# Loading a weight matrix as column halves, a reordered VectorE and an fp32 warm-up in a linear-attention kernel

## The chip, the core and the metric

The kernel runs on one core of a Trainium2 chip. A core has five engines, each with its own in-order instruction stream: TensorE (PE in the profile; its weight loads are PEld), VectorE (DVE), ScalarE (ACT), GpSimd (POOL) and SyncE (SP, which here only issues DMAs). Sixteen DMA engines move data between HBM and the on-chip memories. The metric is the device time of one execution in microseconds (us); lower is better.

## The reference

Input x has 2048 rows of 640 numbers (bf16). Each row is first normalized to xn. The result is x plus two branches of xn:

```python
xn = _layernorm(x)                       # mean and variance over the 640 columns
# A: linear attention with 32 heads of 20
q, k, v = split(xn @ wqkv)
phi = lambda t: where(t > 0, t + 1, exp(t)) + 1e-6
kv  = sum over rows of phi(k)^T v        # one 20x20 matrix per head
z   = sum over rows of phi(k)
A   = ((phi(q) @ kv) / (phi(q) . z + 1e-6)) @ wo
# B: the 8 rows with the largest r = xn @ w_r go through a small MLP
B   = xn, with sigmoid(r) * ((silu(x_sel @ w_gate) * (x_sel @ w_up)) @ w_down) added to those 8 rows
out = x + A + B
```

## The kernel before, in words

The rows are cut into 16 tiles of 128 rows, tile t being rows 128t to 128t+127. The program has a fixed order, written out by hand: every engine runs its instructions in the order in which the Python code emits them, and waits on semaphores for data of the other engines. All loads go through one queue that SyncE issues in order.

**First stage (0 to about 52 us in the profile).** For each tile:

- x arrives by DMA in `XX[:, t, 1, :]`.
- The statistics of a row: `ln_a` and `ln_b` are one `bn_stats` each, over half the columns (L145, L148, VectorE); `ln_g` joins them (L151); `ln_s` (L170, L172) makes the standard deviation with a power on GpSimd. For tiles 1 and 5 ScalarE makes the sums instead (`ln_act`, L159 to L161) and VectorE the variance (`ln_var`, L164).
- `ln_c` (L177 on ScalarE, L179 on VectorE) subtracts the mean, `ln_xn` (L184 a reciprocal, L186 a product) scales and writes the normalized tile.
- The normalized tile is transposed into `xnT`: for tiles 0 to 3 by TensorE, with a copy out of PSUM by ScalarE (`tr_pe`, L193 and L197), from tile 4 on by a DMA (`tr_dma`, L202) that SyncE issues.
- `K(t)` (L224) multiplies by the k weights `wk`: two halves h of 320 columns, 5 products each. The second half has a 321st column that holds w_r, so that r comes out beside k.
- `PHa(t)` (L240, L243, ScalarE) makes exp and relu of both halves, `PHb(t)` (L259, VectorE) joins them into phi(k), `pk`.
- `G(t)` (L264, L269) adds xn^T phi(k) up over the tiles in PSUM.

Tiles 0 to 3 are emitted one by one (L344 to L418); from tile 4 a loop (L419 to L445) emits `K(t)`, `PHb(t-1)`, the normalization of tile t+2, `PHa(t)`, the statistics of tile t+3, and `G(t-1)`. A transposed tile t+2 has thus to be there two rounds of the loop after its normalization was emitted. In the loop the first half statistic stands behind `PHb(t-1)` and ahead of `ln_xn(t+2)` for t = 4 to 8 (tile t+3), and at the round's end for t of 8 and more (tile t+4).

Before the first tile arrives TensorE runs products of zeros (`warm`, L116), and one small transposition of w_r (L127) whose result ScalarE later copies into the 321st column of `wk` (L362, L364). A few lines of the start, with their order:

```python
    ld(sp, XX[:, 2, 1, :], x_v[:, 2, :])
    ld(sp, wk[:, 0:3, 0:D], wqkv_v[:, 0:3, D : 2 * D])
    ld(sp, wk[:, 3:KC, 0:D], wqkv_v[:, 3:KC, D : 2 * D])
    warm(4)
    pe.transpose(PS[:, 5, :].bitcast(BF16)[:, 0:KC], wr[:], ident[0:KC, 0:KC])
    warm(5)
    ld(sp, XX[:, 3, 1, :], x_v[:, 3, :])
```

**Second stage (about 52 us to the end).** The q products (L455) with their exp and relu (L461, L462, L510), the matrices of the heads, the routing of 8 rows through the MLP, and last the output products (L686) tile by tile with the sum and the store (L700, L702). None of this is changed.

Of the kernel before, what the change touches and what calls it, by code (L numbers as in the profile page):

```python
# [7 lines left out]
P = 128  # L8
S = 2048
D = 640  # L10
# [3 lines left out]
T = S // P  # L14
KC = D // P
# [7 lines left out]
FQ = F // 4  # L23
EPS_BF16 = 1.0013580322265625e-05
LOW = S - 1
TF = 11

BF16 = mybir.dt.bfloat16
F32 = mybir.dt.float32
# [7 lines left out]
def kernel(  # L37
# [13 lines left out]
    pe, dve, act, pool, sp = nc.tensor, nc.vector, nc.scalar, nc.gpsimd, nc.sync  # L51

    x_v = A_x[0].rearrange("(t p) d -> p t d", p=P)
    out_v = out[0].rearrange("(t p) d -> p t d", p=P)
    wqkv_v = A_wqkv.rearrange("(kc p) n -> p kc n", p=P)
# [7 lines left out]
    PS = psp.tile([P, 8, 512], F32, name="PS")  # L63

    def st(shape, dt, name, tag=None):
        return sb.tile(shape, dt, name=name, tag=tag or name)

    XX = st([P, T, 2, D], BF16, "XX")
    xnT = st([P, KC, S], BF16, "xnT")
    pk = st([P, T, D], BF16, "pk", "pkwd")  # L70
    pqT = st([P, KC, S], BF16, "pqT")
    wk = st([P, KC, D + 1], BF16, "wk", "wkM")
    wq = st([P, KC, D], BF16, "wq")
    wo1 = st([P, NG, D], BF16, "wo1")
    wo2 = st([P, D], BF16, "wo2")
# [4 lines left out]
    zero = st([P, 512], BF16, "zero")  # L80
    ident = st([P, P], BF16, "ident")
# [12 lines left out]
    MR = st([P, T], F32, "MR")  # L94

    HW = 320


    def ld(eng, dst, src):
        eng.dma_start(dst, src)  # L100
# [5 lines left out]
    wr = st([KC, P], BF16, "wr")  # L106
    ld(act, wr[:], B_w_r.rearrange("(kc p) -> kc p", p=P))
    ld(sp, XX[:, 1, 1, :], x_v[:, 1, :])
    ld(sp, XX[:, 2, 1, :], x_v[:, 2, :])
    ld(sp, wk[:, 0:3, 0:D], wqkv_v[:, 0:3, D : 2 * D])  # L110
    ld(sp, wk[:, 3:KC, 0:D], wqkv_v[:, 3:KC, D : 2 * D])


    def warm(n, w=512):
        for _ in range(n):
            pe.matmul(PS[:, 7, 0:w], lhsT=zero[:, 0:P], rhs=zero[:, 0:w], start=True, stop=True)  # L116
# [6 lines left out]
    )  # L123
    dve.memset(ones32[:], 1.0)
    dve.memset(eps6[:], 1e-6)
    warm(4)
    pe.transpose(PS[:, 5, :].bitcast(BF16)[:, 0:KC], wr[:], ident[0:KC, 0:KC])  # L127
    warm(5)
    ld(sp, XX[:, 3, 1, :], x_v[:, 3, :])
    kv1 = st([P, NG, GC], BF16, "kv1")  # L130
    kv2 = st([P, NG, GC], BF16, "kv2")
    xsT = st([P, KC, 32], BF16, "xsT")
# [10 lines left out]
    def ln_a(t):  # L143
        sts[t] = tmp.tile([P, 2, nc.vector.BN_STATS_DIM], F32, tag="stats", name="stats", bufs=3)
        dve.bn_stats(out=sts[t][:, 0, :], in_=XX[:, t, 1, 0:320])  # L145

    def ln_b(t):
        dve.bn_stats(out=sts[t][:, 1, :], in_=XX[:, t, 1, 320:D])  # L148

    def ln_g(t):  # L150
        dve.bn_aggr(out=MV[:, t, :], in_=sts[t][:])  # L151
# [3 lines left out]
    sm = st([P, T, 2], F32, "sm")  # L155
    junk = st([P, D], BF16, "junk")

    def ln_act(t):
        act.activation(junk[:], XX[:, t, 1, :], AF.Identity, scale=1.0 / D, accum_out=sm[:, t, 0:1])  # L159
        act.copy(MV[:, t, 0:1], sm[:, t, 0:1])  # L160
        act.activation(junk[:], XX[:, t, 1, :], AF.Square, scale=float(D) ** -0.5, accum_out=sm[:, t, 1:2])  # L161

    def ln_var(t):
        dve.scalar_tensor_tensor(out=MV[:, t, 1:2], in0=sm[:, t, 0:1], scalar=sm[:, t, 0:1], in1=sm[:, t, 1:2],  # L164
                                 op0=ALU.mult, op1=ALU.subtract)

    def ln_s(t, sg=1.0):
        t2 = tmp.tile([P, 1], BF16, tag="t2", name="t2", bufs=4)
        ss[t] = tmp.tile([P, 1], BF16, tag="s", name="s", bufs=4)
        dve.tensor_scalar(out=t2[:], in0=MV[:, t, 1:2], scalar1=sg, scalar2=EPS_BF16,  # L170
                          op0=ALU.mult, op1=ALU.add)
        pool.tensor_tensor(out=ss[t][:], in0=t2[:], in1=halfc[:], op=ALU.pow)  # L172

    def ln_c(t, eng):
        cs[t] = tmp.tile([P, D], BF16, tag="c", name="c", bufs=3)
        if eng is act:
            act.activation(cs[t][:], XX[:, t, 1, :], AF.Identity, bias=MVf[:, t, 0:1], scale=-1.0)  # L177
        else:
            dve.tensor_scalar(out=cs[t][:], in0=XX[:, t, 1, :], scalar1=MVf[:, t, 0:1], scalar2=-1.0,  # L179
                              op0=ALU.subtract, op1=ALU.mult)  # L180
# [8 lines left out]
    def tr_pe(t, b0, e0, e1, hs=(0, 1)):  # L189
        for b, k0, k1, eng in [((b0, 0, 3, e0), (b0 + 1, 3, KC, e1))[h] for h in hs]:  # L190
            pt = PS[:, b, :].bitcast(BF16)[:, 0 : (k1 - k0) * P]
            for kc in range(k0, k1):
                pe.transpose(pt[:, (kc - k0) * P : (kc - k0 + 1) * P], XX[:, t, 0, kc * P : (kc + 1) * P], ident[:])  # L193
            dst = xnT[:, k0:k1, t * P : (t + 1) * P]
            src = pt.rearrange("p (k c) -> p k c", c=P)
            if eng is act:
                act.copy(dst, src)  # L197
            else:
                dve.tensor_copy(dst, src)
# [9 lines left out]
    def xpx(t):  # L209
        if t >= TF:  # L210
            dve.tensor_scalar(out=XX[:, t, 1, :], in0=XX[:, t, 1, :], scalar1=SR1[:, t : t + 1],
                              scalar2=MR[:, t : t + 1], op0=ALU.mult, op1=ALU.add)
            return
        act.activation(XX[:, t, 1, :], XX[:, t, 1, :], AF.Identity, bias=MR[:, t : t + 1], scale=SR1[:, t : t + 1])  # L214


    def off(t, h):
        return T - 1 - t if t != 1 and h else 0

    def K(t, hs=(0, 1), b=6, kcs=range(KC)):  # L220
        for h in hs:
            w = HW + h
            for kc in kcs:
                pe.matmul(  # L224
                    PS[:, b + h, off(t, h) : off(t, h) + w],
                    lhsT=xnT[:, kc, t * P : (t + 1) * P],
                    rhs=wk[:, kc, h * HW : h * HW + w],
                    start=(kc == 0),
                    stop=(kc == KC - 1),
                )  # L230
# [3 lines left out]
    def phi_src(t, h, b):  # L234
        return PS[:, b + h, off(t, h) : off(t, h) + HW]

    def PHe(t, h, b=6):
        if h == 0:
            phis[t] = tuple(tmp.tile([P, D], BF16, tag=k, name=k, bufs=3) for k in ("ek", "rk"))
        act.activation(phis[t][0][:, h * HW : (h + 1) * HW], phi_src(t, h, b), AF.Exp)  # L240

    def PHr(t, h, b=6):
        act.activation(phis[t][1][:, h * HW : (h + 1) * HW], phi_src(t, h, b), AF.Relu)  # L243

# [5 lines left out]
    def rcopy():  # L250
        act.copy(rbf[:, 0 : T - 2], PS[:, 7, HW : HW + T - 2])
        dve.tensor_copy(rbf[:, T - 1 : T], PS[:, 7, HW + T - 1 : HW + T])
# [40 lines left out]
    def consts_e():  # L293
        pool.memset(bm2[0:E2, :], 1.0)
        band(bm2[0:E2, :], P, 8)

    def bm2_copies(eng, gs):
        for g in gs:
            ld(eng, bm2[32 * g : 32 * g + 32, :], bm2[0:E2, :])
# [59 lines left out]
    ln_xn(1)  # L359
    ln_g(2)  # L360
    ln_s(2)
    act.copy(wk[:, 0:3, D], PS[:, 5, :].bitcast(BF16)[:, 0:3])  # L362
    K(0, kcs=range(3))
    act.copy(wk[:, 3:KC, D], PS[:, 5, :].bitcast(BF16)[:, 3:KC])  # L364
    tr_pe(1, 2, act, act)
    K(0, kcs=range(3, KC))
    PHe(0, 0)
    consts_e()
    bm2_copies(sp, (1, 2))
    PHr(0, 0)  # L370
    ln_c(2, dve)
    ln_a(3)
    ln_xn(2)
# [45 lines left out]
    for t in range(4, T):  # L419
        K(t)  # L420
        PHb(t - 1)
        if t + 3 < T and t < 9:
            ln_a(t + 3)
        if t + 2 < T:
            ln_xn(t + 2)
            tr_dma(t + 2)
        PHa(t)
        if t + 3 < T:
            ln_b(t + 3)
            ln_g(t + 3)  # L430
            ln_s(t + 3)
            ln_c(t + 3, act)
        if t + 4 < T and t >= 8:
            ln_a(t + 4)
        if t == 13:
            xpx_cols(TF, T)
            xpx(TF)
        if t > 13:
            for i in range(2):
                xpx(TF + 1 + 2 * (t - 14) + i)  # L440
        G(t - 1)
        if t - 1 in pool_extra:
            pool_extra[t - 1]()
        if t > 4:
            loads(t)  # L445
# [19 lines left out]
    for t in range(T - 1):  # L465
# [11 lines left out]
    dve.tensor_scalar(out=rf[:], in0=rbf[:], scalar1=2.0 ** -100, scalar2=None, op0=ALU.add)  # L477
    dve.tensor_scalar(out=sg1[:], in0=rf[:].bitcast(I32), scalar1=31, scalar2=LOW,
                      op0=ALU.arith_shift_right, op1=ALU.bitwise_and)
# [86 lines left out]
    def route2():  # L566
        dve.max(k8[:], krow[:])
        kb = k8[:].bitcast(I32)
        dve.tensor_scalar(out=idx8[:], in0=kb, scalar1=LOW, scalar2=LOW,
                          op0=ALU.bitwise_and, op1=ALU.bitwise_xor)  # L570
        dve.tensor_scalar(out=sg8[:], in0=kb, scalar1=31, scalar2=LOW,
                          op0=ALU.arith_shift_right, op1=ALU.bitwise_and)
# [67 lines left out]
    hs = st([P, FQ], BF16, "hs")  # L640
# [66 lines left out]
    idxh = st([P, 1], I32, "idxh")  # L707
    hi_d = drp.tile([S - TF * P, D], BF16, name="hi_d")
    hi_4 = hi_d[:].rearrange("s (j c) -> (s j) c", j=4)
    hi_v = hi_d[:].rearrange("(t p) d -> p t d", p=P)  # L710
    out_lo = out[0][0 : TF * P, :].rearrange("s (j c) -> (s j) c", j=4)

# [175 lines left out]
```

## Time and profile before

| | |
|---|---|
| median of 3 runs | 113.0 us (112.57 to 113.93) |
| profiled execution | 113.0 us; its instructions span 111.3 us |
| TensorE busy | 103.7 us, 93% of the span |
| VectorE busy | 84.1 us, 76% |
| ScalarE busy | 75.9 us, 68% |
| DMA | 19.04 MB moved |
| chain that ended last | PE 62%, DMA 19%, DVE 9% of the span |

The chain is read from the end of the program backwards: at each step to what released the waiting instruction. Where it names a DMA, an engine waited for that transfer. Starts in the timeline are counted from the first instruction. A weight load or a product that overlaps the one ahead of it counts as busy, so the time that TensorE loses is read from the distance between the starts of its products, not from its busy share. 1.7 us of the execution's 113.0 lie outside the span.

### The profile page before, as it was taken

The numbers are of one execution on the slowest core, as the hardware profiler recorded it, in microseconds if no ns is written. First come the engines' busy times: TensorE is split into PE (matmuls) and PEld (weight loads), VectorE is DVE, ScalarE is ACT, GpSimd is POOL, SyncE is SP. The second block draws the span as 40 slices with busy tenths as digits, with TensorE's granted clock in tenths as the row PEclk, the third lists the DMA queues.
The fourth block names the chain that finished last, engine by engine and source line by source line (L and its number), as shares of the span: only waits on it lengthen the run. The fifth ranks groups of instructions, "written<-read, shape, count | busy, mean of one in ns | idle before, by whom it ended". The sixth has DMA issues, their size and how long they took to land.

```text
span 111.3 us, 2742 instructions
## 1 busy us (share of the span) xinstructions
PE 103.7 (93%) x988; PEld 64.6 (58%) x998; DVE 84.1 (76%) x210; ACT 75.9 (68%) x168; POOL 21.6 (19%) x48
## 2 busy tenths in 40 slices
PE   5968998999999799999999999999999999999970
PEld 1236664666666466667557566565655767777740
DVE  1887987999999977755568976448869898689770
ACT  4626997887888778555496678999979965590000
POOL 7335112367442111000000012200006000000130
PEclk9999999999999999999999999999999999999999
DMA  3899920343356984379999707941721116389442
GB/s 87 231 350 379 238 55 20 62 60 62 66 125 143 77 181 112 66 200 379 358 395 402 276 6 218 382 131 32 251 83 48 32 33 247 62 239 378 162 133 82
DMA packets 22600, 19.04 MB, mean 171 GB/s; under 512 B 11194, under 2 KB 21306, under 8 KB 22586
## 3 DMA queue, kind: packets, MB, share of 16 engines
q1 hardware_dynamic: 21968, 18.69, 58.2%
q8 instruction: 8, 0.13, 0.6%
q10 hardware_dynamic: 330, 0.16, 0.5%
q0 software_dynamic: 288, 0.01, 0.3%
q14 instruction: 6, 0.05, 0.1%
HBM read 13.14 MB, written 3.65 MB: 151 GB/s over the span
## 4 chain that ended last, share of the span: by engine, by line
PE 62%; DMA 19%; DVE 9%; SPq 3%; ACT 2%; issue 2%; POOL 1%; DVEq 0%; ACTq 0%
PE PS L686 20%; PE PS L455 19%; DMA xnT<-XX 8%; PE PS L224 8%; DMA wo<-in_A_wo_dram 6%; PE PS L264 5%; DMA XX<-in_A_x_dram 5%; SPq L100 2%; DVE XX L186 2%; DVE pk L259 2%; PE PS L624 2%; PE PS L630 2%; PE PS L269 1%; PE PS L648 1%; DVE stats L148 1%
## 5 line engine op out<-in xcount | busy, mean ns | idle before, releaser
L224 PE MATMUL PS<-wk,xnT 128*128 128x320 bf16 (+1 forms) x160 | 24.9, 300 | 2.3 <-DMA xnT<-XX 0.9
L455 PE MATMUL PS<-xnT,wq 128*128 128x512 bf16 x95 | 22.8, 380 | 0.3
L264 PE MATMUL PS<-pk,XX 128*128 128x512 bf16 x75 | 22.4, 379 | 0.0
L686 PE MATMUL PS<-Mb,pqT 128*128 128x320 bf16 x160 | 22.1, 299 | 0.0
L224 PEld LDWEIGHTS <-xnT 128*128 128x128 bf16 x160 | 15.2, 97 | 10.3 <-DMA xnT<-XX 1.5
L240 ACT ACTIVATE ek<-PS 128x320 bf16<-128x320 f32 x32 | 14.6, 456 | 7.0 <-PE PS L224 7.0
L686 PEld LDWEIGHTS <-pqT 128*128 128x128 bf16 x160 | 15.5, 97 | 6.4
L172 POOL TENSOR_TENSOR s<-t,halfc 128x1 bf16<-128x1 bf16 x16 | 11.7, 732 | 26.4 <-DVE t L170 26.4
L455 PEld LDWEIGHTS <-wq 128*128 128x128 bf16 x100 | 11.4, 118 | 8.7
L510 DVE SCALAR_TENSOR_TENSOR pqT<-qe,qr 128x512 bf16<-128x512 bf16 x20 | 13.5, 683 | 3.7 <-ACT qr L462 3.7
L461 ACT ACTIVATE qe<-PS 128x512 bf16<-128x512 f32 x20 | 12.2, 608 | 5.5 <-PE PS L455 5.4
L700 DVE TENSOR_TENSOR o<-PS,XX 128x640 bf16<-128x640 f32 x15 | 12.3, 823 | 3.8 <-PE PS L686 2.1
L259 DVE SCALAR_TENSOR_TENSOR pk<-ek,rk 128x640 bf16<-128x640 bf16 x16 | 13.1, 818 | 2.7 <-ACT rk L243 2.7
L243 ACT ACTIVATE rk<-PS 128x320 bf16<-128x320 f32 x32 | 14.6, 458 | 0.0
L269 PE MATMUL PS<-pk,XX 128*128 128x128 bf16 x64 | 14.0, 219 | 0.3
L264 PEld LDWEIGHTS <-XX 128*128 128x128 bf16 x80 | 7.7, 98 | 8.0
L462 ACT ACTIVATE qr<-PS 128x512 bf16<-128x512 f32 x20 | 12.2, 608 | 0.0
L214 ACT ACTIVATE XX<-XX,MR,SR 128x640 bf16<-128x640 bf16 x11 | 9.4, 912 | 2.7 <-DVE pqT L544 2.7
L177 ACT ACTIVATE c<-XX,MVf 128x640 bf16<-128x640 bf16 x10 | 8.3, 832 | 1.2 <-DVE MVf L151 0.9
L145 DVE BATCH_NORM_STATS2 stats<-XX 128x6 f32<-128x320 bf16 x14 | 6.8, 488 | 2.6 <-DMA XX<-in_A_x_dram 2.6
L186 DVE TENSOR_SCALAR XX<-c,SR 128x640 bf16<-128x640 bf16 (+2 forms) x17 | 6.4, 383 | 1.3
L148 DVE BATCH_NORM_STATS2 stats<-XX 128x6 f32<-128x320 bf16 x14 | 6.8, 485 | 0.0
(118 smaller groups left out, 100.2 us busy)
## 6 DMA issues: line engine op xcount, KB each, us to landing
out_dram<-o SPq DMA_DIRECT2D x15, 160.0 KB, 3.3
XX<-in_A_x_dram SPq DMA_DIRECT2D x6, 320.0 KB, 6.4
wg<-in_B_w_gate_dram SPq DMA_DIRECT2D x5, 384.0 KB, 5.6
wu<-in_B_w_up_dram SPq DMA_DIRECT2D x5, 384.0 KB, 7.3
wd<-in_B_w_down_dram SPq DMA_DIRECT2D x1, 1920.0 KB, 9.5
wq<-in_A_wqkv_dram SPq DMA_DIRECT2D x5, 160.0 KB, 2.5
wv<-in_A_wqkv_dram SPq DMA_DIRECT2D x1, 800.0 KB
hi_d<-XX SPq DMA_DIRECT2D x1, 800.0 KB, 5.8
```

Source lines behind the costliest of these rows:

```text
L224: pe.matmul(PS[:, b + h, off(t, h) : off(t, h) + w], lhsT=xnT[:, kc, t * P : (t + 1) * P], rhs=wk[:, kc, h * HW : h * HW + w], start=(kc = ...
L240: act.activation(phis[t][0][:, h * HW : (h + 1) * HW], phi_src(t, h, b), AF.Exp)
L243: act.activation(phis[t][1][:, h * HW : (h + 1) * HW], phi_src(t, h, b), AF.Relu)
L259: dve.scalar_tensor_tensor(out=pk[:, t, :], in0=ek[:], scalar=1.0, in1=rk[:], op0=ALU.min, op1=ALU.add)
L264: pe.matmul(PS[:, a, :], lhsT=lhsT, rhs=pk[:, t, 0:512], start=(t == 0), stop=(t == T - 1),)
L269: pe.matmul(PS[:, 5, a * P : (a + 1) * P], lhsT=lhsT, rhs=pk[:, t, 512:D], start=(t == 0 and a == 0), stop=(t == T - 1), skip_group_check= ...
L455: pe.matmul(PS[:, bank, :], lhsT=by5(wq[:, kc, :])[:, m, :], rhs=xnT[:, kc, tb * TBLK : (tb + 1) * TBLK], start=(kc == 0), stop=(kc == KC ...
L461: act.activation(e, PS[:, bank, :], AF.Exp)
L462: act.activation(r, PS[:, bank, :], AF.Relu)
L510: dve.scalar_tensor_tensor(out=pqT[:, m, tb * TBLK : (tb + 1) * TBLK], in0=e, scalar=1.0, in1=r, op0=ALU.min, op1=ALU.add,)
L686: pe.matmul(PS[:, b + h, 0:HW], lhsT=pqT[:, kc, t * P : (t + 1) * P], rhs=Mb[:, kc, h * HW : (h + 1) * HW], start=(kc == 0), stop=(kc == K ...
L700: dve.tensor_tensor(out=ot[:].rearrange("p (h c) -> p h c", h=2), in0=PS[:, b : b + 2, 0:HW], in1=XX[:, t, 1, :].rearrange("p (h c) -> p h ...
```

## The change

Three things are changed, all in the first stage.

1. The k weights are stored as two column halves, each with its own contiguous region (`wkh`), and each half is one DMA of 5 pieces of 640 bytes to a partition. x of tile 3, which stood behind both parts of the weights in SyncE's queue, stands between the halves. w_r is copied into its column right at the start, in one copy instead of two, ahead of the second half's load; that load waits for the copy. `K(0)` runs its first half, then the transposition of tile 1, then its second half.
2. In the loop the first half statistic of tile t+4 stands at the round's end from t = 4 on, instead of from t = 8 on, so that from t = 5 on `ln_xn(t+2)` follows `PHb(t-1)` directly.
3. Of the ten warm-up products ahead of tile 0, eight of 512 bf16 columns become four of 256 fp32 columns (`warm4`); one of 512 and one of 256 bf16 columns stay. The transposition of w_r goes to another PSUM bank.

The set `ACTS` is empty, so that the branches on it add nothing.

```diff
-    wk = st([P, KC, D + 1], BF16, "wk", "wkM")
+    wk = st([P, KC * (D + 1)], BF16, "wk", "wkM")
+    wkh = [wk[:, 0 : KC * HW].rearrange("p (k c) -> p k c", k=KC),
+           wk[:, KC * HW : KC * (D + 1)].rearrange("p (k c) -> p k c", k=KC)]
...
     ld(sp, XX[:, 2, 1, :], x_v[:, 2, :])
-    ld(sp, wk[:, 0:3, 0:D], wqkv_v[:, 0:3, D : 2 * D])
-    ld(sp, wk[:, 3:KC, 0:D], wqkv_v[:, 3:KC, D : 2 * D])
+    ld(sp, wkh[0], wqkv_v[:, :, D : D + HW])
+    ld(sp, XX[:, 3, 1, :], x_v[:, 3, :])
+    zero32 = zero[:].bitcast(F32)
+    def warm4(n):
+        for _ in range(n):
+            pe.matmul(PS[:, 7, 0:256], lhsT=zero32[:, 0:P], rhs=zero32[:, 0:256], start=True, stop=True)
...
-    warm(4)
-    pe.transpose(PS[:, 5, :].bitcast(BF16)[:, 0:KC], wr[:], ident[0:KC, 0:KC])
-    warm(5)
-    ld(sp, XX[:, 3, 1, :], x_v[:, 3, :])
+    warm4(2)
+    pe.transpose(PS[:, 3, :].bitcast(BF16)[:, 0:KC], wr[:], ident[0:KC, 0:KC])
+    warm4(2)
+    warm(1)
+    act.copy(wkh[1][:, :, HW], PS[:, 3, :].bitcast(BF16)[:, 0:KC])
+    ld(sp, wkh[1][:, :, 0:HW], wqkv_v[:, :, D + HW : 2 * D])
...
-                    rhs=wk[:, kc, h * HW : h * HW + w],
+                    rhs=wkh[h][:, kc, 0:w],
...
-    act.copy(wk[:, 0:3, D], PS[:, 5, :].bitcast(BF16)[:, 0:3])
-    K(0, kcs=range(3))
-    act.copy(wk[:, 3:KC, D], PS[:, 5, :].bitcast(BF16)[:, 3:KC])
+    K(0, (0,))
+    PHe(0, 0)
     tr_pe(1, 2, act, act)
-    K(0, kcs=range(3, KC))
-    PHe(0, 0)
     consts_e()
     bm2_copies(sp, (1, 2))
     PHr(0, 0)
+    K(0, (1,))
     ln_c(2, dve)
...
         PHb(t - 1)
-        if t + 3 < T and t < 9:
+        if t + 3 < T and t < 5 and t + 3 not in ACTS:
             ln_a(t + 3)
...
-        if t + 4 < T and t >= 8:
+        if t + 4 < T and t >= 5 - 1 and t + 4 not in ACTS:
             ln_a(t + 4)
```

## The prediction, made before the changed kernel was run

> **What bounds the kernel now.** I read the page's busy shares first (PE 93%), then the chain in order of time. From 52 us to 107.9 us it is an unbroken row of TensorE products, so a microsecond won or lost before 52 us reaches the end unless something late takes its place. Before 52 us the chain leaves TensorE in few places. Columns: start, us, what.
>
> ```profile
> 3.19 5.62 DMA XX<-in_A_x_dram
> 8.81 0.02 issue
> 8.83 0.49 DVE stats L145
> ...
> 14.89 4.51 DMA xnT<-XX
> 19.40 0.05 issue
> 19.45 1.54 PE PS L224 x10
> ...
> 34.48 4.29 DMA xnT<-XX
> 38.77 0.05 issue
> 38.81 1.54 PE PS L224 x10
> ```
>
> The reader should see three things: x of tile 3 ends the first wait; a VectorE chain then runs to the transposition of tile 4; and two transpositions, of tiles 4 and 11, took 4.51 and 4.29 us, where the view of L202 gives 2.6 for those it can tell. VectorE's timeline shows the first wait, TensorE's the second:
>
> ```profile
> 7.81 0.38 DVE L179 TENSOR_SCALAR c<-XX,MVf 128x640 bf16<-128x640 bf16 x1
> 8.83 0.49 DVE L145 BATCH_NORM_STATS2 stats<-XX 128x6 f32<-128x320 bf16 x1 [0.65 <-DMA XX<-in_A_x_dram]
> ...
> ```
> ```profile
> 18.71 0.38 PE L264 MATMUL PS<-pk,XX 128*128 128x512 bf16 x1
> 19.45 0.45 PE L224 MATMUL PS<-wk,xnT 128*128 128x320 bf16 x2 [0.36 <-DMA xnT<-XX]
> ```
>
> A 512-column product is followed after 0.22 us, so K(4) was due at 18.93 and lost 0.52. K(11) was due at 38.13 (35.46 + 2.67, the distance of all other rounds: 19.45, 22.12, 24.79 ...) and lost 0.68. So the loop is paced by TensorE, not VectorE, but for these two stalls. Why were these two transpositions slow? The DMA view of 17.2 to 17.4 us has one packet, and that of 35.6 to 35.8 one of the same kind among the transposition's own:
>
> ```profile
> q8 instruction: 1, 0.02, 28.8%
> ```
> ```profile
> q8 instruction: 1, 0.02, 46.5%
> ```
>
> 28.8% of 16 engines' 0.2 us is 0.92 us on one DMA engine, 46.5% is 1.49 us. I read them as code packets, which hold up one of the 16 engines while a transposition needs all. The first came at the end of tile 4's (14.89 + 2.6 = 17.49), the second at the start of tile 11's data.
>
> A page of the Trainium skill, "Runtime: NRT & Kernel Launch" (Instruction fetch mechanics), speaks against this: code comes in 16 KiB blocks of 256 instructions, and crossing one is "mostly hidden". The 8 packets of 0.13 MB agree with it for some 1,986 PE instructions; the two long transpositions don't agree with "hidden". By the page alone the stalls would have another cause and stay, which is the second rival below.
>
> **x of tile 3 between the halves.** 800 KB of weights stand ahead of it now, 400 KB then. The windows view has 373 GB/s from 8 to 12 us, so 400 KB are 1.1 us: landing at 7.7 instead of 8.81. Pieces of 640 bytes aren't in the trace. Bounds: no dearer per byte, or each as dear as one of 1,280 (a half then takes 2.2 us, x lands at 8.8, and the later half holds K(4) 0.1 us longer than now). The nearest rows are the 3,072-byte loads at 54 to 56 us, 398 GB/s: 2.4 times smaller pieces cost 6%, so I take 0.1 us for each half, x at 7.8. VectorE is busy until 8.14 anyway, and then the power of tile 2 on POOL (7.97 + 0.62 = 8.59) holds its reciprocal: 8.62 against 9.24. From there the chain is VectorE's own, so tile 4's transposition is issued **0.62 us earlier**, at 14.27. x of tiles 4 and 5, due 0.2 later (9.9), is needed at 10.24.
>
> **K(0) as halves.** First half: now 480 KB let it start at 7.55, then 400 KB, about 7.3; 5 steps of 0.137 (chain: 1.37 for 10) to 8.0; the transposition of tile 1 to 8.3. The second half lands when now all 800 KB and x have, 8.81, plus 0.2: products from 9.05, K(1)'s first half from 9.74, tile 2's transposition from 10.42 (now 10.68), its copies at 10.8 behind ScalarE's relu (now 11.37), K(2) at 11.4 (now 11.97). Were the half 0.2 later still, K(2) would be at 11.55. TensorE then runs unbroken, as it does now from 11.97, to the end of G(2): 18.93 less 0.42 to 0.57, **18.4 to 18.5**.
>
> **K(4).** Its transposition, undisturbed, lands at 14.27 + 2.6 = 16.87. The code packet moves with TensorE to 16.8 to 16.96: a tie. If it misses, K(4) starts at 18.45 (gain 1.0); if it hits with the same 1.9 us, at 18.83 (gain 0.62). I take **0.8**, and keep both ends.
>
> **The wait in SyncE's queue.** The second half now waits for ScalarE's copy, that for w_r's transposition (3.06, 0.18 us): issue at about 3.5 instead of 3.15. Six x loads are queued behind it. Cover: until 7.8 the DMA engines work on what was issued before, so the wait costs nothing before it is 4 us longer; ScalarE is idle until 3.65, so its copy costs nothing.
>
> **VectorE's order.** No instruction more. L145 ahead of the reciprocal took 0.53 (25.29 to 25.82), behind L170 0.40 (32.67 to 33.07): VectorE's round falls from 2.7 to 2.53. That alone is worth nothing while TensorE's 2.67 paces. What it moves is `ln_xn` and so the DMA's issue. With relu(8) ending at 32.04 + 0.46 = 32.50, PHb(8) can start then instead of at 33.07 and tile 11's transposition is issued at 33.9 instead of 34.48. Undisturbed it lands at 36.5. The code packet stays where TensorE's program has it, 35.70: now ahead of the last 0.8 us of the transposition instead of all of it. Delayed by 1.7 to 1.9 (what the two cases cost), it lands at 38.2 to 38.4 against 38.13 due, so 0.05 to 0.3 is lost instead of 0.68: **gain 0.55** (0.4 to 0.68).
>
> **Warm-up.** Eight products of 512 columns, 0.427 us each (1.24 to 3.06 holds four), are replaced by four. The only fp32 row is this; the chain gives it 0.11 us, two passes of the 0.055 that a 128-column bf16 transposition (L193) takes:
>
> ```profile
> L547 PE MATMUL PS<-identf,key x1: 272/272/272, 56.5 to 56.5; 128*16 128x128 f32 x1
> ```
>
> Two for the moving side, and two again for a stationary side in fp32, is 4 × 0.213 = 0.85 each at the start's half speed: 3.4 us as before, cost 0. Bounds: 0.43 (moving side alone) to 1.7. Shorter costs nothing by itself; at 1.7, 3.1 us more before tile 0's transposition, of which some 1.1 are covered (0.3 idle ahead of it, the waits for both halves). As two load-and-product pairs each, they leave the code packets at their place; as one pair, these come some 0.5 us later, which only helps.
>
> **Sum.** 113.0 (the profiled execution; also the median of the runs) - 0.8 - 0.55 = **111.6 us**. A measurement here tells no less than about 2%, 2.26 us, from no change; TensorE alone can't reach that: its gaps to be won are 0.57 + 0.52 + 0.68 = 1.8.
>
> **Rivals.**
>
> - *Both stalls go, and the start is at its best* (packets miss): 113.0 - 1.1 - 0.7 = 111.2, and 111.0 if the smaller pieces cost nothing, since the second half then lands 0.2 earlier. For: packet 1 was within 0.1 us of missing. Against: packet 2 needs 0.6 more. Chance 0.30.
> - *Code isn't the cause, or the later transposition isn't earlier since ScalarE holds PHb*: only the 0.6 remains, 112.4. For: the page's rule. Against: the DMA view of 17.5 to 19.4 us is all but empty. Chance 0.12.
> - *The start isn't earlier*, 640-byte pieces being dear, or tile 5's statistics on ScalarE hold K(5) (due 21.6, needed 22.12, slack 0.5): 112.4. Chance 0.08.
> - *Slower: TensorE's full speed comes late.* Now it comes before 7.55 (three 320-column products in 0.57). If the fp32 products count for less activity, products run at half speed until a time X; what is done before 9.05 is covered by the wait for the second half, each us after it costs half: 113.0 - 1.35 + (X - 9.05) / 2. Slower than now from X = 11.8; 114.1 at X = 14, 2% at 16.3. Against: the array is as long in use as before. Chance 0.12. The Trainium skill, "TensorE: Matmul & The Clock Gate" (What's actually happening), has a free-running window of 3.4 us that must be busy; by it X would move in steps of that size, and no row here shows how fp32 counts.
>
> **Chances and range.** Forecast 0.38, rivals 0.30, 0.12, 0.08, 0.12. 2% faster is 110.74: of the best case, which lies 0.3 to 0.5 above it, I give somewhat under half (runs spread by 0.4 to 0.9 around their median), of the forecast a tenth: 0.18. 2% slower: of the late clock three quarters, 0.09. Within: 0.73. The range takes in the best case and the two at 112.4 with the runs' spread: 110.6 to 113.2.
>
> **What would show it.** L145 of tile 3 without idle time, at 8.15; K(2) near 11.4, K(4) at 18.4 to 18.85; K(11) within 0.3 of its due time; tile 11's DMA issued about 1.1 us after K(9) instead of 1.7; L116 and the fp32 line ending before 5.7. Wrong if K(2) is later than 11.97, if the three first products of K(0) take 1 us instead of 0.57, or if another transposition takes over 4 us and K waits for it.

## The result, and the profile after

| | before | changed |
|---|---|---|
| median of 21 runs | 112.57 us (111.82 to 113.93) | 112.02 us (111.73 to 115.35) |
| ratio of the times, 95% interval | | 0.9953 [0.9932, 0.9975] |
| profiled execution (span) | 113.0 us (111.3) | 112.53 us (110.8) |

The change makes the kernel faster by 0.5%, 0.55 us in the medians and 0.5 in the profiled executions. The forecast was 111.6 us, 1.4 less than the profile of before. The direction is right, the size is about a third of it. (Some executions, many of them with a lower granted clock, take over 1.5% longer than their kernel's fastest; the ratios leave them out and the medians don't, so the two can differ.)

The chain in order of time, of the changed kernel; columns: start, us, what. L156 is the half statistic (L145 before), L241 is K (L224 before).

```profile
1.71 3.63 DMA XX<-in_A_x_dram
5.33 0.02 issue
5.36 0.49 DVE stats L156
...
14.98 4.27 DMA xnT<-XX
19.25 0.05 issue
19.30 1.54 PE PS L241 x10
...
33.82 4.44 DMA xnT<-XX
38.26 0.05 issue
38.31 1.55 PE PS L241 x10
```

x of tile 3 has left the chain. In its place stands x of tile 2, which landed at 5.33. But the two long transpositions, of tiles 4 and 11, are still there, 4.27 and 4.44 us. K(4) starts at 19.30 (before 19.45), K(11) at 38.31 (38.81). From there on both kernels take the same time: the last long row of output products starts at 89.58 after and at 90.05 before. So 0.15 us of the gain came at K(4), 0.35 at K(11), and nothing was lost or won later.

VectorE's timeline of the changed kernel (start, us, line, operation; in brackets the idle time ahead of it and its releaser):

```profile
5.36 0.49 DVE L156 BATCH_NORM_STATS2 stats<-XX 128x6 f32<-128x320 bf16 x1 [0.63 <-DMA XX<-in_A_x_dram]
5.77 0.15 DVE L201 RECIPROCAL SR<-s 128x1 f32<-128x1 bf16 x1
...
8.63 0.49 DVE L156 BATCH_NORM_STATS2 stats<-XX 128x6 f32<-128x320 bf16 x1
```

The half statistic of tile 3, at 8.63, has no idle time ahead of it any more: that wait is gone as forecast. But 0.63 us of idle time stand ahead of tile 2's at 5.36, and tile 0's reciprocal, next in VectorE's order, waits behind it although its power was done at 5.16. So tile 2's reciprocal starts at 9.15 where 8.62 was forecast, its product then takes 0.56 us (0.39 before), and tile 4's transposition is issued at 14.98, after 14.89 before, instead of at 14.27. TensorE is earlier: K(2) starts at 11.27 instead of 11.97.

TensorE's timeline of the changed kernel, its warm-up, K(0)'s second half and the two stalls:

```profile
1.24 2.07 PE L121 MATMUL PS<-zero 128*128 128x256 f32 x4 [1.24 <-DVE MVf L108]
...
8.93 1.26 PE L241 MATMUL PS<-wk,xnT 128*128 128x321 bf16 x8 [0.23 <-DMA wk<-in_A_wqkv_dram]
...
18.13 0.38 PE L281 MATMUL PS<-pk,XX 128*128 128x512 bf16 x1
...
19.30 0.58 PE L241 MATMUL PS<-wk,xnT 128*128 128x320 bf16 x3 [0.79 <-DMA xnT<-XX]
...
37.81 0.38 PE L281 MATMUL PS<-pk,XX 128*128 128x512 bf16 x1
...
38.31 0.58 PE L241 MATMUL PS<-wk,xnT 128*128 128x320 bf16 x3
```

A 512-column product is followed after 0.22 us: K(4) was due at 18.35 and came at 19.30, 0.95 late (before: 0.52). K(11) was due at 38.03 and came at 38.31, 0.28 late (before: 0.68). So TensorE reached K(4) 0.58 us earlier, and 0.43 of that went into a longer wait for the same transposition.

The code packets, by the DMA view of 17.1 to 17.4 us and of 35.6 to 35.9 us:

```profile
q8 instruction: 1, 0.02, 19.2%
```
```profile
q8 instruction: 1, 0.02, 26.7%
```

19.2% of 16 engines' 0.3 us are 0.92 us on one engine, 26.7% are 1.28. The first packet came at 17.23, 2.25 us after the transposition's issue, and so fell inside it; the second came at 35.70, inside tile 11's. In the profile of before the first came at 17.38: it moved by 0.15 us, as much as K(4).

### The profile page after: what moved, and what is told of

It reads as the page before. It is cut to its first block, busy times and chain, and to the rows that moved or that the text cites. A ratio compares the mean times of both kernels' runs of the same rounds, so it can differ in the third digit from the quotient of the medians.

```text
span 110.8 us, 2749 instructions
## 1 busy us (share of the span) xinstructions
PE 104.8 (95%) x998; PEld 66.3 (60%) x998; DVE 84.5 (76%) x210; ACT 75.3 (68%) x167; POOL 20.3 (18%) x48
## 3 DMA queue, kind: packets, MB, share of 16 engines
HBM read 13.14 MB, written 3.65 MB: 152 GB/s over the span
## 4 chain that ended last, share of the span: by engine, by line
PE 73%; DMA 11%; DVE 7%; POOL 2%; ACT 1%; issue 1%; SPq 1%; DVEq 0%; ACTq 0%
PE PS L708 20%; PE PS L477 20%; PE PS L241 12%; PE PS L281 10%; DMA xnT<-XX 8%; DMA XX<-in_A_x_dram 3%; DVE XX L203 2%; POOL s L189 2%; PE PS L286 2%; PE PS L646 2%; PE PS L652 2%; PE PS L670 1%; DVE pk L276 1%; PE PS L540 1%; PE PS L300 1%
## 5 line engine op out<-in xcount | busy, mean ns | idle before, releaser
L241 PE MATMUL PS<-wk,xnT 128*128 128x320 bf16 (+1 forms) x160 | 24.8, 301 | 1.1 <-DMA xnT<-XX 0.8
L281 PE MATMUL PS<-pk,XX 128*128 128x512 bf16 x80 | 23.2, 379 | 0.0
L241 PEld LDWEIGHTS <-xnT 128*128 128x128 bf16 x160 | 15.4, 98 | 8.9 <-DMA xnT<-XX 1.6
L477 PEld LDWEIGHTS <-wq 128*128 128x128 bf16 x100 | 11.4, 118 | 8.7
L189 POOL TENSOR_TENSOR s<-t,halfc 128x1 bf16<-128x1 bf16 x16 | 9.8, 610 | 27.3 <-DVE t L187 27.3
L281 PEld LDWEIGHTS <-XX 128*128 128x128 bf16 x80 | 7.7, 98 | 8.1
L156 DVE BATCH_NORM_STATS2 stats<-XX 128x6 f32<-128x320 bf16 x14 | 6.8, 486 | 2.5 <-DMA XX<-in_A_x_dram 2.5
L286 PEld LDWEIGHTS <-XX 128*128 128x128 bf16 x64 | 6.2, 97 | 1.0 <-issue 0.2
```

Of the source, the lines that this page charges most:

```text
L241: pe.matmul(PS[:, b + h, off(t, h) : off(t, h) + w], lhsT=xnT[:, kc, t * P : (t + 1) * P], rhs=wkh[h][:, kc, 0:w], start=(kc == 0), stop=( ...
L281: pe.matmul(PS[:, a, :], lhsT=lhsT, rhs=pk[:, t, 0:512], start=(t == 0), stop=(t == T - 1),)
L286: pe.matmul(PS[:, 5, a * P : (a + 1) * P], lhsT=lhsT, rhs=pk[:, t, 512:D], start=(t == 0 and a == 0), stop=(t == T - 1), skip_group_check= ...
L477: pe.matmul(PS[:, bank, :], lhsT=by5(wq[:, kc, :])[:, m, :], rhs=xnT[:, kc, tb * TBLK : (tb + 1) * TBLK], start=(kc == 0), stop=(kc == KC ...
```

## The experiments

The theory to be tested is that of the prediction: a code packet that lies inside a transposition lengthens it from 2.6 to over 4 us, and K waits. Its rivals are that the long transposition has another cause, and that the gain comes from one part of the change alone. In the tables "due" is the start of the last 512-column product ahead of K(4) or K(11) plus 0.22.

### Each part alone, and the changed kernel again

The loads and K(0) alone (the changed kernel with VectorE's old order and the bf16 warm-up):

```diff
-        if t + 3 < T and t < 5 and t + 3 not in ACTS:
+        if t + 3 < T and t < 9 and t + 3 not in ACTS:
...
-        if t + 4 < T and t >= 5 - 1 and t + 4 not in ACTS:
+        if t + 4 < T and t >= 8 and t + 4 not in ACTS:
...
-    warm4(2)
+    warm(4)
...
-    warm4(2)
-    warm(1)
+    warm(5)
```

> Part 1 alone (column halves, x of tile 3 between them, early copy of w_r; bf16 warm-up and the old VectorE order). Theory A, that the start's gain is real but is eaten at K(4), since the transposition of tile 4 isn't issued earlier and meets a code packet: x of tile 3 there before VectorE wants it (no idle time ahead of its L145 statistic), K(2) at 11.2 to 11.6, K(4) ready on TensorE at 18.4 but started at 18.8 to 19.4, K(11) late by 0.5 to 0.7 as in the kernel before; 0 to 0.4 us faster than before. Rival, that the weights' order alone makes the whole measured gain: 0.5 us or more faster, and part 2 alone nothing.

VectorE's order alone, put into the kernel before:

```diff
-        if t + 3 < T and t < 9:
+        if t + 3 < T and t < 5:
...
-        if t + 4 < T and t >= 8:
+        if t + 4 < T and t >= 4:
```

> Part 2 alone (the half statistic of tile t+4 at the round's end from t = 4 on). Theory A: everything up to K(4) as before; the transposition of tile 11 is issued about 1.1 us after K(9) starts instead of 1.7, so K(11) loses 0.1 to 0.3 us against the distance of the other rounds instead of 0.68; 0.3 to 0.6 us faster than before. Rival, that TensorE paces the loop and the order does nothing: 0.0, and K(11) late by 0.7 as before.

The fp32 warm-up alone, put into the kernel before:

```diff
+    zero32 = zero[:].bitcast(F32)
+
+    def warm4(n):
+        for _ in range(n):
+            pe.matmul(PS[:, 7, 0:256], lhsT=zero32[:, 0:P], rhs=zero32[:, 0:256], start=True, stop=True)
...
-    warm(4)
+    warm4(2)
...
-    warm(5)
+    warm4(2)
+    warm(1)
```

> Part 3 alone (fp32 warm-up). Theory A: no change, within 0.2 us; two fp32 products end at 2.95 to 3.15 (four bf16 ones at 2.93), the first products of K(0) still 0.137 us apart. Rival, that the fp32 warm-up brings TensorE's full speed earlier or later: the transpositions of tile 0 at 0.055 us instead of 0.107, or K(0)'s products at 0.27 us, and a time off by more than 0.3 us.

The changed kernel with the bf16 warm-up only taken back:

```diff
-    warm4(2)
+    warm(4)
...
-    warm4(2)
-    warm(1)
+    warm(5)
```

> The changed kernel with the bf16 warm-up of the kernel before (parts 1 and 2 alone). Theory A: fp32 is worth nothing, time within 0.2 us of the changed kernel, the same stall at K(4). Rival: fp32 steadies the clock at the start, and without it executions over 113 us come back in one of five, as with the kernel before.

The changed kernel once more, without an edit:

> The changed kernel once more, unchanged, beside the others on one chip: 0.4 to 0.6 us below the kernel before; the first code packet 2.1 to 2.5 us after the issue of tile 4's transposition, and K(4) 4.1 to 4.6 us after it, 0.4 to 1.0 us late.

Measured (the first three beside one set of runs of the kernel before, median 112.5; the last two beside another, 112.35):

| kernel | median us | ratio, 95% | x3 landed | tile 4's transposition issued | K(4) due, started | K(11) late by |
|---|---|---|---|---|---|---|
| loads and K(0) | 112.09 | 0.9982 [0.9960, 1.0005] | 7.44 | 14.36 | 18.19, 18.57 | 0.18 |
| order | 112.22 | 0.9989 [0.9954, 1.0025] | 8.02 | 14.56 | 18.13, 18.91 | 0.07 |
| fp32 warm-up | 112.42 | 0.9992 [0.9962, 1.0021] | 9.27 | 15.35 | 19.38, 19.91 | 0 |
| changed, bf16 warm-up | 111.87 | 0.9980 [0.9955, 1.0004] | 7.13 | 14.43 | 17.99, 18.75 | 0.06 |
| changed, again | 111.65 | 0.9944 [0.9921, 0.9967] | 6.51 | 14.44 | 17.81, 18.74 | 0 |

What follows. The whole change is worth 0.5% in two independent comparisons. Each part alone is worth 0.1 to 0.2% with an interval that holds 1, so none can be told from nothing by itself, and their sum, 0.4%, can't be told from the 0.5% of the whole. Whether the fp32 warm-up gives a part of the 0.5% stays open: with bf16 back the median is 0.2 us higher (eleven of the changed kernel's twelve runs are at or below 111.77 us, two of the twelve with bf16), but the intervals overlap, K(4) starts at the same time in both profiles, and alone the fp32 warm-up shows nothing. Its rival, executions over 113 us with bf16, fell: none of the twelve is over 112.5.

The traces say more than the times. K(11)'s stall isn't there in every execution of the old order. TensorE's timeline of the fp32 warm-up alone, which has the old order:

```profile
38.37 0.38 PE L271 MATMUL PS<-pk,XX 128*128 128x512 bf16 x1
38.59 1.26 PE L231 MATMUL PS<-wk,xnT 128*128 128x320 bf16 x8
```

K(11) follows after 0.22 us, without a wait. The DMA view of 35.9 to 36.2 us of that kernel has its packet:

```profile
q8 instruction: 1, 0.02, 20.8%
```

That is 1.0 us on one engine, where the profile of before had 1.49, and the transposition took 3.60 us where it had 4.29. In both K(11) is due 3.65 us after the issue, so the shorter one is just covered and the longer one is not. The old order lost 0.68, 0.18 and 0 in three profiles, and 0.89 in a fourth, that of the last experiment below, whose execution was its kernel's slowest. The new order does what it was said to do: tile 11's DMA is issued 1.14 us after K(9) in the changed kernel and 1.15 with the order alone, instead of 1.68. K(11) is then due 4.2 us after the issue, and the four profiles with the new order in this table and the result have it 0 to 0.28 late. What that is worth on the average the times don't settle: 0.1% alone, with an interval that holds 1.

And x of tile 2 lands anywhere between 4.1 and 5.3 us, whatever stands behind it in the queue: 4.81 before, 5.33 changed, 4.14 changed again, 4.51 with the loads alone, 4.90 with the order alone. That the changed kernel's profile had it late is chance. In the second profile of the changed kernel, with x2 at 4.14, K(4) comes at 18.74, 0.71 earlier than in the profile of before, which is near the 0.8 forecast. But there too it is 0.94 late, and the packet had come 0.70 earlier, at 16.68.

### Moving the code packet

If the packet is the cause, K(4) must come on time when the packet lies elsewhere. Later by fewer instructions ahead of it: two fp32 products of 512 columns in place of four of 256, eight TensorE instructions fewer.

```diff
-            pe.matmul(PS[:, 7, 0:256], lhsT=zero32[:, 0:P], rhs=zero32[:, 0:256], start=True, stop=True)
+            pe.matmul(PS[:, 7, :], lhsT=zero32[:, 0:P], rhs=zero32[:, 0:256].unsqueeze(1).to_broadcast([P, 2, 256]), start=True, stop=True)
...
-    warm4(2)
+    warm4(1)
...
-    warm4(2)
+    warm4(1)
     warm(1)
```

> The changed kernel with its four fp32 warm-up products of 256 columns drawn together into two of 512: as much time, but 8 TensorE instructions fewer ahead of everything that follows, so that code packets come about 0.55 us later against TensorE's work. Theory C (a code packet on one DMA engine is what makes the transposition of tile 4 long): the first packet, at 17.2 us in the changed kernel's profile, comes near 17.8, after an undisturbed transposition has landed (issue + 2.6, so 17.0 to 17.6); the transposition then takes 2.6 to 3 us and K(4) starts at its due time 18.2 to 18.4 in most executions; about 0.6 to 0.9 us faster than the changed kernel. Rival D (the first transposition behind the loads is long by itself): 4.2 to 4.5 us from issue to K(4) as in all five kernels so far, time within 0.2 us of the changed kernel's.

Earlier by more instructions: three of the four fp32 products as bf16 products of 128 columns, 36 instructions more.

```diff
-    warm4(2)
+    warm(16, 128)
...
-    warm4(2)
+    warm(8, 128)
+    warm4(1)
     warm(1)
```

> The changed kernel with three of its four fp32 warm-up products replaced by eight bf16 products of 128 columns each: as much time, but 36 TensorE instructions more, so that code packets come about 2.4 us earlier against TensorE's work. Theory C: the first packet near 14.8 us, before the transposition of tile 4 has data under way (issue + 1.2, about 15.8); the transposition takes 2.6 to 3 us, K(4) starts at its due time 18.2 to 18.4; the second packet, near 33.3, falls on the transposition of tile 10 instead of 11, which has about 1.5 us to spare; 0.6 to 0.9 us faster than the changed kernel. Rival D: K(4) 4.2 to 4.5 us after the issue, no change.

The first packet later and the other packets back where they were: the long fp32 products as above, and four products of K(5) cut in two, which gives the eight instructions back behind the first packet.

```diff
             for kc in range(KC):
-                pe.matmul(
-                    PS[:, b + h, off(t, h) : off(t, h) + w],
...
-                    rhs=wkh[h][:, kc, 0:w],
...
+                cuts = (0, HW // 2, w) if t == 5 and h == 0 and kc > 0 else (0, w)
+                for c0, c1 in zip(cuts, cuts[1:]):
+                    pe.matmul(
+                        PS[:, b + h, off(t, h) + c0 : off(t, h) + c1],
...
+                        rhs=wkh[h][:, kc, c0:c1],
...
```

> The changed kernel with two fp32 warm-up products of 512 columns for the four of 256 (8 TensorE instructions fewer), and, behind the first code packet, four products of K(5) cut into two of 160 columns (8 instructions more), so that only the first code packet comes later and all others stand where the changed kernel has them. Theory C (the first packet holds up tile 4's transposition, and moving the others starved or hit other work in the runs that moved all of them): K(4) within 0.1 us of its due time, 18.0 to 18.5; no gap of TensorE behind it; 0.6 to 1.0 us faster than the changed kernel, near 111.1 us. Rival G (the two long fp32 products themselves, or an early clock, make the slow executions of the runs with the later packets): some executions over 113 us again.

| kernel | median us | ratio, 95% | issue of tile 4's transposition | packet after it by | K(4) due, started | K(11) late by |
|---|---|---|---|---|---|---|
| changed | 112.02 | 0.9953 [0.9932, 0.9975] | 14.98 | 2.25 | 18.35, 19.30 | 0.28 |
| code later | 112.57 | 0.9922 [0.9869, 0.9974] | 14.38 | 2.65 | 18.44, 18.44 | 0 |
| code earlier | 112.00 | 0.9954 [0.9909, 0.9998] | 14.79 | -0.06 | 18.15, 18.15 | 0 |
| first packet later | 111.60 | 0.9939 [0.9911, 0.9966] | 14.46 | 3.03 | 18.21, 18.21 | 0.23 |

TensorE's timeline of "code later":

```profile
18.23 0.38 PE L281 MATMUL PS<-pk,XX 128*128 128x512 bf16 x1
18.44 0.84 PE L241 MATMUL PS<-wk,xnT 128*128 128x320 bf16 x5
```

and of "code earlier":

```profile
17.93 0.38 PE L282 MATMUL PS<-pk,XX 128*128 128x512 bf16 x1
18.15 0.84 PE L242 MATMUL PS<-wk,xnT 128*128 128x320 bf16 x5
```

K(4) follows its predecessor without a wait in both. The packets, by the DMA view of 17.0 to 17.3 us of "code later" and of 14.7 to 15.0 us of "code earlier":

```profile
q8 instruction: 1, 0.02, 21.8%
```
```profile
q8 instruction: 1, 0.02, 25.1%
```

Over all 14 profiles of this study: in the eight with the packet 2.15 to 2.49 us behind the transposition's issue K(4) was late, by 0.38 to 1.06 us; in the six with the packet 2.60 us or more behind it, or ahead of it, K(4) was on time. Where the packet fell inside, the trace's records have 15 of the transposition's 16 parts landed within 2.7 us of the issue, and the last one after 4.2 to 4.5; where it missed, all had landed within 2.9. In all eight the last part landed 1.10 us after the packet's end, whatever the transposition's issue, and K(4) started 2.06 to 2.11 us after the packet's start. So in these the packet's time sets K(4)'s. The code packet is the cause of the stall at K(4): shown, by moving the packet both ways.

Two things besides speak for it. In "code earlier" the second packet fell into tile 10's transposition (packet at 31.60, issue at 30.28), the tile that was expected, and that one took 3.93 us, while tile 11's took 2.80; K(10) had time to spare and was 0.06 late. And a packet of 8 KB of another code queue, 0.31 to 0.42 us long, fell 1.92 to 2.03 us behind the issue of tile 8's transposition in ten profiles: the last part landed after 3.20 to 3.22 us in all ten, and after 2.56 to 2.67 in the other four. K(8) was on time all the same. One case goes the other way: in the last kernel of the next section a packet fell 2.42 us behind the issue of tile 11's transposition, which still took 2.63. Eight instructions move the packet only loosely, though. It came 0.7 to 1.4 us ahead of K(4)'s due time in the four kernels that have eight fewer ahead of it, and 1.0 to 1.7 in the eight stalled ones; of the kernels made for it, only the earlier one, 3.4 ahead, stands clear.

The Trainium skill, "Runtime: NRT & Kernel Launch" (Instruction fetch mechanics), calls the cost of crossing a 16 KiB block of code "mostly hidden". For TensorE's own stream that holds at these two places; for the DMA transposition of tile 4 that runs at the same time the measurement decides: 1.6 to 1.9 us longer.

Yet the time hardly followed. "First packet later" beats the kernel before by 0.6%, the changed kernel beside it, in the same set of runs, by 0.56%: 111.60 against 111.65. Its K(4) is 0.53 us earlier than that of the changed kernel's second profile, but K(11) only 0.18 and the last output row 0.17 (88.56 against 88.73). TensorE's timeline of "first packet later" at K(11):

```profile
36.84 0.38 PE L283 MATMUL PS<-pk,XX 128*128 128x512 bf16 x1
37.29 1.54 PE L243 MATMUL PS<-wk,xnT 128*128 128x320 bf16 x10
```

Its DMA view of 34.8 to 35.1 us:

```profile
q8 instruction: 1, 0.02, 20.6%
```

The next packet, 1.0 us long at 34.92, fell inside tile 11's transposition (issued 33.05), and K(11) was 0.23 late. Another 0.1 went into the rounds between, K(4) to the due time of K(11), which hold the cut products: 18.85 us instead of 18.73. So of 0.53 us saved at the first packet two thirds came back as a wait at the next packet and as the cost of the cuts. Rival G fell: none of the twelve runs is over 112.25 us, where three of the six of "code later" and two of the six of "code earlier" are over 113. K(0)'s second half of weights also landed later in the four kernels with the long products (8.8 to 9.3, against 8.2 to 8.9), though its load is issued at the same time as in the changed kernel, 3.67; whether the long products do that or chance stays open.

### Tile 0's reciprocal ahead of tile 2's statistic

The profile of the changed kernel showed tile 0's reciprocal held by x of tile 2. Here it goes first.

```diff
-    ln_a(2)
     ln_xn(0, ((0, 3 * P), (3 * P, D)))
...
     ln_c(1, dve)
+    ln_a(2)
     ln_b(2)
```

> The changed kernel with the first half statistic of tile 2, which waits for x of tile 2, moved from ahead of tile 0's normalization to ahead of tile 2's second half statistic. In the changed kernel's profile x of tile 2 landed at 5.33 us and tile 0's reciprocal, whose power was done at 5.16, stood behind it until 5.77. Theory A: the reciprocal at 5.2 to 5.3, the transposition of tile 4 issued 0.3 to 0.5 us earlier than 14.98, and since TensorE's place at the code packet doesn't move, the packet misses it more often: K(4) at 18.4 to 18.9 instead of 19.30; 0.3 to 0.8 us faster than the changed kernel. Rival, that x of tile 2 isn't what counts (the load of the second weight half is): tile 4's transposition not earlier and the time within 0.2 us of the changed kernel's.

Measured: 112.01 us (111.75 to 112.34), ratio 0.9972 [0.9950, 0.9994], no faster than the changed kernel. VectorE's timeline:

```profile
5.15 0.16 DVE L201 RECIPROCAL SR<-s 128x1 f32<-128x1 bf16 x1 [0.47 <-POOL s L189]
...
6.40 0.49 DVE L156 BATCH_NORM_STATS2 stats<-XX 128x6 f32<-128x320 bf16 x1
```

TensorE's:

```profile
17.78 0.38 PE L281 MATMUL PS<-pk,XX 128*128 128x512 bf16 x1
19.06 0.72 PE L241 MATMUL PS<-wk,xnT 128*128 128x320 bf16 x4 [0.90 <-DMA xnT<-XX]
```

The wait went (the reciprocal at 5.15, behind its own power), and K(2) came 0.56 us earlier than in the changed kernel, at 10.71. Tile 4's transposition was issued 0.34 earlier, at 14.64. But the packet came earlier with TensorE, at 17.00 instead of 17.23, 2.36 us behind the issue, and K(4) was 1.06 late. The expectation that an earlier transposition would slip past the packet fell: both the packet and the transposition hang on the same start and move together. K(4) started 2.06 us after the packet here too.

The same edit together with the moved packet:

> The kernel with only the first code packet later, and tile 2's first half statistic moved out of the way of tile 0's normalization. Theory C: K(4) at its due time with more to spare than without the move; 0.6 to 1.1 us faster than the changed kernel. If the statistic's place matters by itself, another 0.1 to 0.2 us below the kernel with the later packet alone.

111.64 us (111.08 to 112.49), ratio 0.9930 [0.9898, 0.9961]; K(4) on time at 18.65, K(11) 0.22 late. It can't be told from the same kernel without the edit (0.9939).

And with all packets later, the kernel of "code later" with this edit:

> The kernel with the later code packets and tile 2's first half statistic out of the way of tile 0's normalization. Theory C: tile 4's transposition is issued at 14.4 to 14.7 and lands by 17.0 to 17.3, the packet comes at 17.5 to 17.6: misses with 0.3 us to spare, K(4) at 18.0 to 18.3, 0.8 to 1.0 us faster than the changed kernel. Rival D: as the changed kernel.

115.19 us (110.94 to 115.58 over six runs). K(4) was on time at 18.12, but TensorE's timeline has this, much later in the program:

```profile
57.85 0.38 PE L300 MATMUL PS<-pk,ones 128*32 128x160 bf16 x10
60.40 1.61 PE L300 MATMUL PS<-pk,ones 128*32 128x160 bf16 x54 [2.16 <-issue]
```

The view by windows of the same kernel (time, then busy us and instructions of PE, PEld, DVE, ACT and POOL, granted clock, DMA share, GB/s):

```profile
57.50:60.91 3.41, 1.25 (x107) 1.05 (x98) 2.84 (x9) 0.94 (x2) 0.00 (x0) 1.00 1.03 395
60.91:64.32 3.41, 3.41 (x44) 1.67 (x33) 1.02 (x2) 0.02 (x1) 0.00 (x0) 0.50 0.12 38
```

In the midst of a row of 64 equal products TensorE stood for 2.16 us with nothing that it waited for, and its granted clock was then 0.50 from 60.91 to 64.32. A code packet was fetched only at 57.93 here, 0.08 us behind the row's start, where the other kernels have it 3.3 to 5.6 us ahead of that row; the DMA engines moved 395 GB/s at the time. That TensorE had run out of code is the reading that fits these rows; nothing was run to test it alone. It may bear on "code later" too, whose six runs reach up to 115.32 us and which shifts every packet alike; its own profile doesn't show it.

### The order of the loads alone

x of tile 3 between the two parts of the weights, which stay cut by rows as before.

```diff
-    ld(sp, wk[:, 3:KC, 0:D], wqkv_v[:, 3:KC, D : 2 * D])
+    ld(sp, XX[:, 3, 1, :], x_v[:, 3, :])
+    ld(sp, wk[:, 3:KC, 0:D], wqkv_v[:, 3:KC, D : 2 * D])
...
-    ld(sp, XX[:, 3, 1, :], x_v[:, 3, :])
```

> The kernel before with only x of tile 3 moved between the two loads of the weights, which stay cut by rows, in pieces of 1,280 bytes. Theory E (the queue's order makes the start's gain, not the column halves): x of tile 3 lands about 0.7 to 0.9 us earlier than in the kernel before (8.0 to 9.3 in three profiles), tile 4's transposition is issued 0.2 to 0.5 us earlier, but K(0) still waits for all of the weights (8.8 to 9.2) for half its products. Time 0.1 to 0.4 us below the kernel before. Rival F (the halves matter, K(0) holds everything): no change.

Measured: 112.67 us (111.96 to 114.64), ratio 1.0024 [0.9976, 1.0072]; its profiled execution took 114.64. Its TensorE timeline:

```profile
7.58 0.57 PE L224 MATMUL PS<-wk,xnT 128*128 128x320 bf16 x3 [1.08 <-DMA wk<-in_A_wqkv_dram]
9.14 0.81 PE L224 MATMUL PS<-wk,xnT 128*128 128x321 bf16 x3 [0.99 <-ACT wk L364]
```

Its view by windows:

```profile
5.92:9.33 3.41, 1.35 (x11) 0.78 (x11) 3.19 (x14) 0.98 (x4) 1.84 (x5) 1.00 1.03 360
9.33:12.74 3.41, 3.41 (x18) 2.13 (x17) 2.29 (x9) 2.17 (x6) 0.91 (x2) 0.50 1.33 352
```

x3 landed at 7.94, as wanted, but TensorE then has two waits close together, 1.08 us for the first part of the weights and 0.99 for ScalarE's copy into the second part. A stretch at half speed follows, 9.33 to 12.74 us, and K(2) starts only at 13.68. No gain of the order of the loads by itself shows in the times. Why not, this profile can't tell: the other five runs, 111.96 to 113.41 us, are faster than the one that it shows. With halves by columns K(0) does its five products early and the transposition of tile 1 with them. No profile with column halves has such a stretch at the start, but neither have the other three with halves by rows, so that the halves prevent it isn't shown.

The Trainium skill, "TensorE: Matmul & The Clock Gate" (What's actually happening), has the clock checked in free-running windows of 3.4 us. The 3.41 us of half speed agree. It has the throttle return after an idle window; here the 3.41 us ahead of the fall weren't idle, TensorE was busy for 1.35 us of them, a share of 0.40. In the section above, in the kernel whose clock fell at 60.91, it was 1.25 us, or 0.37. Full speed began there at 6.30, 54.61 us or 16 times 3.41 earlier. Cut into such stretches from the moment at which full speed began, the 14 traces have no other one up to 105 us with a share under 0.53 (the fp32 warm-up alone, 1.80 us from 6.56 to 9.97), and the clock fell after no other.

## Why the prediction was right in part

Point by point, by its own steps:

- **What bounds the kernel** held: TensorE from 52 us on without a change, two stalls at K(4) and K(11), and the code packet as their cause. The rival "code isn't the cause" fell with the kernels that move the packet.
- **x of tile 3 between the halves** held for the load: x landed at 6.90 instead of 7.8, its statistic had no wait left, and pieces of 640 bytes cost nothing that shows. What it was to bring, tile 4's transposition 0.62 us earlier, did not come: 14.98 in this profile, 14.44 in the kernel's second.
- **K(0) as halves** held: K(2) at 11.27 (11.4 said), TensorE ready for K(4) at 18.35 (18.4 to 18.5 said), full speed by K(0)'s second half at the latest (eight products in 1.26 us, 0.137 apart).
- **K(4)** failed, and is the mis-sized term: 0.8 us said, 0.15 found in the profile. Its lower end (the packet hits) was priced at 0.62. Two things were missing. The transposition was issued at 14.98 instead of 14.27, mainly since x of tile 2 came 0.52 later than in the profile of before and VectorE's fixed order passed that on; the working took 4.81 for a constant where 4.1 to 5.3 is its spread. And the hit was priced as a fixed 1.9 us from the transposition's issue on, while the last part lands 1.10 us after the packet's end. The packet came at 17.23, not at 16.8 to 16.96 as said, and so K(4) came only 0.15 earlier; TensorE, ready 0.58 earlier, waited longer, 0.95 instead of 0.52.
- **The wait in SyncE's queue** held: the second half was issued at 3.67 (3.5 said).
- **VectorE's order** held in the mechanism (1.14 us from K(9) to the DMA) and in the profile (K(11) 0.28 late, 0.05 to 0.3 said; 0.4 won where 0.55 stood in the sum). The reason given, that the packet would hold up only the last 0.8 us of the transposition, did not hold: all 16 parts came late, 4.24 to 4.44 us after the issue (before 4.09 to 4.29), and what was won is the earlier issue. On the average it may be worth less, 0.1% alone, since the 0.68 of before isn't the rule: the same old order lost 0, 0.18 and 0.89 in three other profiles.
- **Warm-up** held: each fp32 product is two load-and-product pairs, and two products take 2.07 us where four bf16 ones take 1.89, which delays w_r's copy and with it the second half's load (3.67, with bf16 3.49); no cost shows alone (0.9992).
- **The base** was too high. 113.0 was the profile's time and the median of three runs; 21 runs, these three among them, have 112.57, and two later sets 112.5 and 112.35. The sum subtracted stalls that the profiled execution had and another may have in part. Between the two profiled executions the gain was 0.5 us where 1.35 stood in the sum: 0.65 of the shortfall is K(4), 0.2 is K(11). That the changed kernel's second median, 111.65, all but equals the forecast is luck: the kernel before had 112.35 beside it, 0.65 under the base.

## What to carry to other kernels

Before a stall of the profile is put into a sum, look for it in a second profile: a collision of two transfers that take turns by chance is worth its average, not what one execution shows. When a stall comes from something that moves along with the engine that waits (here the code of TensorE's own program), starting everything earlier doesn't remove it; only moving one against the other does, and then the next packet has to be looked at too. Ask also what the landing hangs on: here it was the packet's end, not the transposition's issue. Whether loads cut so that the first product can start on the first piece are worth more than the same loads in another order isn't shown: 0.9982 and 1.0024, with intervals that overlap.

## What the runs showed of the hardware

- A 16 KB code packet of the first stage takes 0.92 to 1.5 us. Tile 4's transposition, with the packet 2.15 to 2.49 us behind its issue, takes 4.2 to 4.5 us instead of 2.6, and only the last of its 16 parts is late. Tile 11's, with the packet 1.0 to 2.1 us behind it, takes 3.6 to 4.4, and all 16 are late but in one profile. At tile 4 the last part lands 1.10 us after the packet has ended in eight of eight profiles (18.15 and 19.25 in the changed kernel), so the packet's own time is not all of the delay; what the rest is stays open.
- The first loads of a program land with a spread of over a microsecond from one execution to another (x of tile 2 at 4.14 to 5.33 us in kernels that issue it alike), and an in-order VectorE hands that on to the whole first stage.
- TensorE's clock changed at whole numbers of 3.41 us after it had first risen. In 14 traces two stretches of that length up to 105 us had TensorE busy for a share of 0.37 and 0.40, and half speed followed for 3.41 us; the next lowest, 0.53, was followed by full speed.
- A change of a few instructions at the start shifts every later fetch of code; in one kernel TensorE then stood for 2.16 us within a row of equal products 50 us later (cause argued, not tested).
